# Attention and two feed-forward layers on one core: signs restored by a bit, a shorter weight split, pooling placed by the plan

## The chip, the cores and the metric

The kernel runs on one NeuronCore of one Trainium2 chip. The number that counts is the device time of one execution in microseconds (us); a run's profile shows the span, from the first to the last instruction of the core, which is slightly shorter. Engines are named as in the profile: PE (TensorE, matmuls), PEld (its weight loads), DVE (VectorE), ACT (ScalarE), POOL (GpSimd) and SP (SyncE, whose queue issues all DMAs here).

## The reference

Three layers follow each other on 4608 tokens (8 batches of 576). Inputs are of both kinds: q, k and v are 32-bit floats, the weights come as 64-bit floats.

```python
k_p = k.reshape(B, H, 72, 8, 64).mean(axis=3)        # pool keys and values by 8
v_p = v.reshape(B, H, 72, 8, 64).mean(axis=3)
attn = softmax(q @ k_p.T / 8)                        # 8 heads of 64
x = (attn @ v_p)  -> [4608, 512]
h = x @ w_in                                         # 512 -> 1024
solu = h * softmax(h)
ln = (solu - mean) / sqrt(var + 1e-6) * g_ln
x = ln @ w_out                                       # 1024 -> 512
h = x @ w2_in                                        # 512 -> 2048
out = (h * sigmoid(1.702 * h)) @ w2_out              # 2048 -> 512
```

## The kernel before, in words

The program has two parts. The first does attention and the first layer (w_in, w_out), and prepares the weights of the second layer (w2_in, w2_out) beside them; its 18 pairs of 128-token tiles leave their result in DRAM (y_dram). The second part runs the second layer over 12 blocks of 384 tokens, with a scheme of seven products in place of eight; its instruction order is written out by hand and the diff doesn't touch it. Every fp32 operand of a matmul is held as a high and a low fp16 half, so that each product is three passes.

**The weights.** They arrive as 64-bit words, in tiles called raw with the two 32-bit words of each number side by side: hw, the high word, and lw, the low word. A fp32 value is put together from them in pieces of 128x512. In `joined` (first layer) and `values_of` (second layer) ACT takes the sign of the high word (tile sg, fp16), converts the low word, and rescales the high word; DVE shifts and joins the two into a positive fp32 word; and POOL multiplies by the sign. The first layer has 16 such pieces, 8 of w_in and 8 of w_out. For these `first_half` then has ACT scale the value into a tile val, ACT write its high fp16 half (tile w1i or w1o), and POOL or DVE subtract to get the low half. The second layer has 32 pieces in 16 quarters (`Quarter`): there POOL's product goes into w_f, out of which POOL makes sums and differences, ACT the high and POOL the low halves, and SP stores both to DRAM. The sign tiles come from a ring of four (SG).

**The pooling.** `half` loads one half of a batch's keys or values (tile half, 128x2x72x8) and `total` adds each group of eight: on DVE it is one reduction, on POOL three additions of halves. The table KV_POOL sends two of the 32 halves to POOL: the second half of keys 0 and the second of values 1.

**Each tile of attention** goes through psx (scores, PE), a maximum, a subtraction, an exponential and a sum (DVE and ACT on tile e), a product with the reciprocal (POOL or DVE), a split into st (ACT and POOL), a DMA transpose into aT, the product with the values in PSUM tile psv (PE), and its split into xT (ACT and DVE). **The first layer** goes through psh (PE, xT times w1i), a maximum, an exponential, a product (tt) and a square on DVE and ACT, statistics on POOL (q, r, a, mean), a split into zs (ACT and POOL), a DMA transpose into zT, psy (PE, zT times w1o), and y.

**The order in the first part** is made by a planner in the kernel's own code (class `Plan`) as the program is built. Each piece of work is a strand, a generator that yields operations with a cost for each engine that may take it. Over and over the planner takes the operation that could begin first by its clocks (one for each engine in `plan.free`, one for the DMAs), shifted a little by its due time, and emits it; the engines then work in that order. V, A, G mean DVE, ACT and POOL alone; VG lets the planner choose between POOL and DVE, with 3000 ns against DVE; `there` emits nothing and holds a strand until its data are there by the planner's clocks. A changed cost or engine therefore changes the order of all that follows in the first part.

Of the kernel before, what the change touches and what calls it, by code (L numbers as in the profile page):

```python
# [8 lines left out]
F32 = mybir.dt.float32  # L9
F16 = mybir.dt.float16  # L10
I32 = mybir.dt.int32
U32 = mybir.dt.uint32
AF = mybir.ActivationFunctionType
ALU = mybir.AluOpType
# [4 lines left out]
P = 128  # L19
# [18 lines left out]
UW = 256  # L38
WC = 512
# [29 lines left out]
DUE_MAX_IN = -10000  # L69
DUE_MAX_OUT = 20000  # L70

RAWS = 4
SG = 4
TTS = 4
V_TOP = 2.0 ** 14

TOP3 = 2.0 ** -29 * (1 - 2.0 ** -23)
A_TOP = 2.0 ** 14
LN_UP = 2.0 ** 10
CI_LEAST, CI_MOST = 2.0 ** -50, 2.0 ** 40  # L80
# [11 lines left out]
NS = 7  # L92
# [79 lines left out]
class Plan:  # L172
# [30 lines left out]
    def drop(self, *tiles):  # L203
        for t in tiles:
            del self.ring_of[t.name]
# [75 lines left out]
def moe_kernel(ctx: ExitStack, tc: tile.TileContext, qT, kT, vT, w_in, w_out, g_ln, w2_in, w2_out, eye, outT):  # L281
# [135 lines left out]
    with ExitStack() as ph:  # L417
# [4 lines left out]
        kv = tc.alloc_tile_pool(name="kv", bufs=2, side="right")  # L422
# [12 lines left out]
        plan = Plan()  # L435
        start, drop = plan.start, plan.drop
# [4 lines left out]
        def there(*ins):  # L441

            return Op(("none",), lambda engine: None, [], ins, {"none": 0})
# [46 lines left out]
        def V(name, *args, **kw):  # L490
            return op(("dve",), name, args, kw)

        def G(name, *args, **kw):
            return op(("pool",), name, args, kw)

        def VG(name, *args, **kw):
            return op(("pool", "dve"), name, args, kw)

        def A(**kw):
            return op(("act",), "activation", (), kw)  # L500
# [89 lines left out]
        def values_of(raw, up, dst, begun=None):  # L590

            hw, lw = raw[:, :, 1], raw[:, :, 0]
            sg = yield New(kv, [P, WC], F16, "sg", bufs=SG)
            if begun is not None:
                begun.append(sg)
            yield A(out=sg, in_=hw.bitcast(F32), func=AF.Sign)
            yield A(out=lw.bitcast(U32), in_=lw.bitcast(U32), func=AF.Copy, scale=TOP3, bias=-0.49999)
            yield lambda: (up.name, up.offset) in upped
            yield A(out=hw.bitcast(F32), in_=hw.bitcast(F32), func=AF.Copy, scale=up)
            yield V(  # L600
                "scalar_tensor_tensor", out=lw, in0=hw, scalar=3, in1=lw, op0=ALU.logical_shift_left,
                op1=ALU.bitwise_or,
            )
            d = yield from dst()
            yield G("tensor_tensor", out=d, in0=sg, in1=lw.bitcast(F32), op=ALU.mult)
            drop(sg)

        def raw_new(q, n):
            return New(kv, [P, q, n, 2], I32, "raw", "raw", RAWS)

# [19 lines left out]
        def joined(raw, measured):  # L630
# [3 lines left out]
            yield A(out=sg, in_=hw.bitcast(F32), func=AF.Sign)  # L634
            yield A(out=lw.bitcast(U32), in_=lw.bitcast(U32), func=AF.Copy, scale=TOP3, bias=-0.49999)
            yield measured
# [8 lines left out]
        def first_half(raw, measured, scaled, up, k, c, his):  # L645

            yield from joined(raw, measured)
            yield scaled
            val = yield New(kv, [P, NS, UW], F32, "val", "w_f", 2)
            v = val.rearrange("p s f -> p (s f)")[:, :WC]  # L650
            hi, lo = (x[:, k, c] for x in his)
            yield A(out=v, in_=raw[:, :, 0].bitcast(F32), func=AF.Copy, scale=up)
            yield A(out=hi, in_=v, func=AF.Copy)
            yield VG("tensor_tensor", out=lo, in0=v, in1=hi, op=ALU.subtract)
            drop(val)

        def halves(n):
            return [slice(j * WC, (j + 1) * WC) for j in range(n // WC)]
# [73 lines left out]
            scaled = start(scale(), due)  # L732
            yield until(*[start(part(i), due + 4 * i) for i in range(n)])

        KV_POOL = {("k", 0): 1, ("v", 1): 1}

        def spans(t):

# [7 lines left out]
        def total(engine, out, x):  # L746

            if engine is V:
                yield V("tensor_reduce", out=out, in_=x, axis=AX.X, op=ALU.add)
                return  # L750
            for n in (4, 2):
                yield G("tensor_tensor", out=x[..., 0:n], in0=x[..., 0:n], in1=x[..., n : 2 * n], op=ALU.add)
            yield G("tensor_tensor", out=out, in0=x[..., 0], in1=x[..., 1], op=ALU.add)
# [4 lines left out]
        def half(kind, b, j, src, dst):  # L758

            raw = yield New(kv, [P, 2, SP, NPOOL], F32, "half", bufs=3)  # L760
            begun[kind][b] += 1
            yield D(raw.rearrange("p a s o -> p a (s o)"), src[b][:, 2 * j : 2 * j + 2])
            yield from total(G if KV_POOL.get((kind, b)) == j else V, dst[:, 2 * j : 2 * j + 2], raw)
            drop(raw)

        def pooled(kind, b, src, due):
# [48 lines left out]
        def attention(t):  # L815
# [42 lines left out]
            yield V("tensor_reduce", out=rs, in_=e, axis=AX.X, op=ALU.add)  # L858
            yield A(out=rs, in_=rs, func=AF.Copy, scale=1.0 / A_TOP, bias=1e-9 / A_TOP)
            yield V("reciprocal", rs, rs)  # L860
# [33 lines left out]
            turned_x = ps.rearrange("p (k t) -> p k t", t=P)  # L894
            yield A(out=xT[:, 0:KM], in_=turned_x, func=AF.Copy, scale=1.0 / A_TOP)
            yield V(
# [270 lines left out]
        begun = {kind: [0] * B for kind in "kv"}  # L1167
# [18 lines left out]
        def due(t):  # L1186
            return FIRST_STEP + STEP * t
# [21 lines left out]
        for b in range(1, B):  # L1209
            d = due(b * S // P + LEAD_KV) if b > 1 else DUE_KV1  # L1210
# [13 lines left out]
        for u in range(len(chunks) // 2):  # L1224
            d = FIRST_STEP + LAG_W2 + 2 * u * STEP_W2
# [254 lines left out]
```

## Time and profile before

| what | us |
|---|---|
| median of 3 runs | 1255.61 |
| lowest and highest run | 1253.86, 1258.69 |
| profiled execution, its own time | 1253.29 |
| profiled execution, its span | 1251.5 |
| granted TensorE clock, mean of the span | 0.986 |
| PE busy in the span | 1143.5 (91%) |
| ACT, DVE, POOL busy in the span | 766.5, 730.9, 664.7 |

Busy time is the sum of an engine's instructions in a stretch; what is left of the stretch is idle time. A row of the waits says who stood still, for whom, how long in total, how often, and the longest time. In a row of the timeline or of the groups the part in brackets, or after the second bar, is the idle time of that engine just before the instruction, and what ended it.

### The profile page before, as it was taken

Reading aid. Unit: us, or ns where it says so; the run is one execution under the profiler, and the core shown is the slowest. Engines: PE = TensorE matmul, PEld = TensorE weight load, DVE = VectorE, ACT = ScalarE, POOL = GpSimd, SP = SyncE. Lnnn points to the kernel's source line nnn. Section 1 sums busy time; section 2 is a strip of 40 time slices with the busy share of each in tenths; the row PEclk is TensorE's granted clock in tenths of the full one; section 3 lists DMA queues with packets and bytes.
Section 4 is the critical chain, followed back from the end, with each engine's and each line's share of the span. In section 5 each row is a group of like instructions: output and inputs, shape, how many; then the busy total and the mean of one; then the engine's idle time right before and its main releaser. Section 6 shows DMA issues by size and latency. Waiting matters only on the chain.

```text
span 1251.5 us, 27586 instructions
## 1 busy us (share of the span) xinstructions
PE 1143.5 (91%) x11678; PEld 989.6 (79%) x11678; DVE 730.9 (58%) x1153; ACT 766.5 (61%) x1073; POOL 664.7 (53%) x696
## 2 busy tenths in 40 slices
PE   2778998899999999889999999999999999999998
PEld 2335665576666666789999999999999898999998
DVE  7898877587677843136455454637272737364543
ACT  6998998788789855345445353627263536454552
POOL 5887998687879953424333352525262515243331
PEclk9989999899999999999999999999999999999999
DMA  9979999999989698470101010100011010101000
GB/s 324 302 205 240 269 270 256 248 231 248 256 206 234 164 230 236 109 270 8 46 14 39 14 40 20 33 27 27 27 33 46 7 46 8 46 7 46 14 14 26
DMA packets 246524, 152.85 MB, mean 122 GB/s; under 512 B 163584, under 2 KB 226176, under 8 KB 244096
## 3 DMA queue, kind: packets, MB, share of 16 engines
q1 hardware_dynamic: 246400, 151.09, 45.5%
q8 instruction: 91, 1.49, 0.5%
q14 instruction: 33, 0.27, 0.1%
HBM read 77.66 MB, written 33.55 MB: 89 GB/s over the span
## 4 chain that ended last, share of the span: by engine, by line
PE 30%; POOL 12%; DVE 8%; ACT 8%; issue 5%; DMA 0%; ACTq 0%; POOLq 0%
PE bank_a L1290 18%; PE bank_d L1290 8%; ACT w_g L1325 6%; DVE g L1337 5%; POOL w_g L336 3%; PE bank_b L1290 3%; POOL w_g L335 3%; POOL w_g L333 2%; POOL w_g L334 2%; PE psy L512 2%; ACT g L1334 1%; DVE c L1303 1%; POOL zs L475 1%; DVE w_g L333 0%; ACT c L1300 0%
## 5 line engine op out<-in xcount | busy, mean ns | idle before, releaser
L1290 PEld LDWEIGHTS <-w2i 128*128 128x128 f16 x4032 | 337.4, 98 | 34.3 <-issue 33.7
L1290 PEld LDWEIGHTS <-w2o 128*128 128x128 f16 x4032 | 335.0, 98 | 7.4 <-issue 6.8
L333 POOL TENSOR_TENSOR w_g<-w_g 128x384 f32<-128x384 f32 x36 | 43.6, 1211 | 379.3 <-ACT w_g L1325 379.3
L1290 PE MATMUL bank_a<-ys,w2i 128*128 128x192 f16 x2304 | 215.1, 247 | 27.1 <-ACT c L1300 25.0
L512 PE MATMUL psh<-w1i,xT 128*128 128x512 f16 x864 | 205.8, 389 | 8.9 <-DVE mean L475 8.2
L1290 PE MATMUL bank_a<-g,w2o 128*128 128x192 f16 x2304 | 206.0, 246 | 1.0
L512 PE MATMUL psy<-zT,w1o 128*128 128x256 f16 x1728 | 196.8, 273 | 8.8 <-ACT y L475 8.8
L512 PEld LDWEIGHTS <-w1o 128*128 128x128 f16 x1728 | 167.9, 98 | 35.8 <-issue 10.3
L1337 DVE SCALAR_TENSOR_TENSOR g<-w_g,gu_b,g 128x1152 f16<-128x1152 f32 (+1 forms) x96 | 169.1, 1782 | 24.5 <-ACT g L1334 24.4
L512 PEld LDWEIGHTS <-xT 128*128 128x128 f16 x864 | 84.4, 100 | 103.9 <-issue 13.8
L1300 ACT ACTIVATE c<-bank_a 128x384 f32<-128x384 f32 x192 | 91.7, 484 | 116.4 <-PE bank_a L1290 113.1
L1334 ACT ACTIVATE g<-w_g,gu_b 128x1152 f16<-128x1152 f32 (+1 forms) x96 | 132.9, 1408 | 39.4 <-POOL w_g L336 39.0
L1303 DVE SCALAR_TENSOR_TENSOR c<-bank_d,c 128x384 f32<-128x384 f32 x96 | 53.3, 555 | 134.4 <-ACT c L1300 99.5
L475 POOL TENSOR_TENSOR zs<-tt,zs 128x1024 f16<-128x1024 f32 x36 | 77.4, 2149 | 59.7 <-ACT zs L475 59.5
L1290 PE MATMUL bank_d<-ys,w2i 128*128 128x192 f16 x1152 | 107.5, 249 | 0.3 <-DVE c L1303 0.3
L1290 PE MATMUL bank_d<-g,w2o 128*128 128x192 f16 x1152 | 102.4, 246 | 3.0 <-DVE g L1337 3.0
L1325 ACT ACTIVATE w_g<-c,ch_b 128x1536 f32<-128x1536 f32 x48 | 75.3, 1568 | 36.8 <-DVE c L1303 36.7
L1300 ACT ACTIVATE c<-bank_a,co_b 128x384 f32<-128x384 f32 x47 | 26.9, 573 | 108.6 <-PE bank_a L1290 108.6
L512 PE MATMUL psx<-kbd,qt 128*128 128x144 f32 (+1 forms) x320 | 46.3, 306 | 24.6 <-ACT raw_z L475 12.7
L512 PEld LDWEIGHTS psx<-kbd,qt 128*128 128x128 f32 (+1 forms) x320 | 41.4, 193 | 29.4 <-issue 12.7
L475 POOL TENSOR_TENSOR lo<-w_f,hi 128x512 f16<-128x512 f32 (+1 forms) x46 | 62.2, 1365 | 2.7 <-ACT hi L475 2.3
L475 DVE TENSOR_REDUCE hmx<-psh 128x1 f32<-128x1024 f32 x36 | 43.7, 1214 | 34.1 <-PE psh L512 34.1
(189 smaller groups left out, 1693.1 us busy)
## 6 DMA issues: line engine op xcount, KB each, us to landing
raw<-w_out SPq DMA_DIRECT2D x12, 1024.0 KB, 6.9
raw<-w_in SPq DMA_DIRECT2D x10, 1024.0 KB, 8.0
half<-kT SPq DMA_DIRECT2D x16, 576.0 KB, 5.4
half<-vT SPq DMA_DIRECT2D x16, 576.0 KB, 5.5
qt<-qT SPq DMA_DIRECT2D x36, 256.0 KB, 3.9
y_dram<-y SPq DMA_DIRECT2D x36, 256.0 KB, 2.8
y<-y_dram SPq DMA_DIRECT2D x48, 192.0 KB, 3.2
outT<-c SPq DMA_DIRECT2D x48, 192.0 KB, 1.9
```

What stands on the lines that cost most here:

```text
L333: eng.tensor_tensor(out=w[:, 1], in0=q[:, Q12], in1=q[:, Q11], op=ALU.subtract)
L334: eng.tensor_tensor(out=w[:, 2], in0=q[:, Q22], in1=w[:, 1], op=ALU.subtract)
L335: eng.tensor_tensor(out=w[:, 0], in0=q[:, Q22], in1=q[:, Q12], op=ALU.subtract)
L336: eng.tensor_tensor(out=w[:, 3], in0=q[:, Q21], in1=w[:, 2], op=ALU.subtract)
L475: getattr(eng, name)(*args, **kw)
L512: nc.tensor.matmul(*p[:3], start=p[3], stop=p[4])
L1290: nc.tensor.matmul(bank[:, q], self.weight(p, q, kk, w), self.data(p, kk, i), start=(first and q == 0 and kk == 0 and w == 0 and i == 0), ...
L1300: nc.scalar.activation(out=self.c[:, i], in_=bank, func=AF.Copy, scale=self.scale)
L1303: nc.vector.scalar_tensor_tensor(out=self.c[:, i], in0=bank, scalar=self.scale, in1=self.c[:, i], op0=ALU.mult, op1=ALU.add)
L1325: nc.scalar.activation(out=self.w[:, 0:4], in_=self.c, func=AF.Gelu_apprx_sigmoid, scale=self.ch)
L1334: nc.scalar.activation(out=self.g[:, 0, s], in_=self.w[:, s], func=AF.Copy, scale=self.gu)
L1337: nc.vector.scalar_tensor_tensor(out=self.g[:, 1, s], in0=self.w[:, s], scalar=self.gu, in1=self.g[:, 0, s], op0=ALU.mult, op1=ALU.subtract,)
```

## The change

- In `values_of` (second layer) the sign tile, ACT's sign instruction and POOL's multiplication go. In their place DVE takes the sign bit of the rescaled high word, joins it to the positive word, and writes w_f. `joined` (first layer) keeps the sign tile and the multiplication.
- In `first_half` the tile val goes: ACT writes the high half straight from the joined word with the scale, and DVE alone writes the low half from the joined word, the scale and the high half, in one instruction.
- The second half of values 1 is no longer fixed to POOL. For all batches after the first, `half` waits until its data are there by the planner's clocks and then takes POOL if POOL's clock plus 1300 ns lies before DVE's, and DVE otherwise.

```diff
+POOL_MORE = 1300
...
+SIGN = -(2 ** 31)
...
         def values_of(raw, up, dst, begun=None):
 
             hw, lw = raw[:, :, 1], raw[:, :, 0]
-            sg = yield New(kv, [P, WC], F16, "sg", bufs=SG)
             if begun is not None:
-                begun.append(sg)
-            yield A(out=sg, in_=hw.bitcast(F32), func=AF.Sign)
+                begun.append(True)
             yield A(out=lw.bitcast(U32), in_=lw.bitcast(U32), func=AF.Copy, scale=TOP3, bias=-0.49999)
...
             d = yield from dst()
-            yield G("tensor_tensor", out=d, in0=sg, in1=lw.bitcast(F32), op=ALU.mult)
-            drop(sg)
+
+            yield V(
+                "scalar_tensor_tensor", out=d.bitcast(I32), in0=hw, scalar=SIGN, in1=lw, op0=ALU.bitwise_and,
+                op1=ALU.bitwise_or,
+            )
...
             yield from joined(raw, measured)
             yield scaled
-            val = yield New(kv, [P, NS, UW], F32, "val", "w_f", 2)
-            v = val.rearrange("p s f -> p (s f)")[:, :WC]
             hi, lo = (x[:, k, c] for x in his)
-            yield A(out=v, in_=raw[:, :, 0].bitcast(F32), func=AF.Copy, scale=up)
-            yield A(out=hi, in_=v, func=AF.Copy)
-            yield VG("tensor_tensor", out=lo, in0=v, in1=hi, op=ALU.subtract)
-            drop(val)
+            v = raw[:, :, 0].bitcast(F32)
+            yield A(out=hi, in_=v, func=AF.Copy, scale=up)
+            yield V("scalar_tensor_tensor", out=lo, in0=v, scalar=up, in1=hi, op0=ALU.mult, op1=ALU.subtract)
...
-        KV_POOL = {("k", 0): 1, ("v", 1): 1}
+        KV_POOL = {("k", 0): 1}
...
-            yield from total(G if KV_POOL.get((kind, b)) == j else V, dst[:, 2 * j : 2 * j + 2], raw)
+            yield there(raw)
+            free = plan.free["pool"] + POOL_MORE < plan.free["dve"]
+            yield from total(G if (b == 0 and KV_POOL.get((kind, b)) == j) or (b and free) else V, dst[:, 2 * j : 2 * j + 2], raw)
```

## Rows read from the trace of the kernel before

**Rows 1.** The page, part 1: busy time, share of span, instructions by engine.

```profile
PE 1143.5 (91%) x11678; PEld 989.6 (79%) x11678; DVE 730.9 (58%) x1153; ACT 766.5 (61%) x1073; POOL 664.7 (53%) x696
```

**Rows 2.** Busy times by stretch: length, PE, PEld, DVE, ACT, POOL, clock, DMA.

```profile
31.00:125.00 94.00, 70.75 (x491) 40.86 (x491) 82.19 (x157) 85.43 (x143) 75.57 (x88) 0.91 0.96 249
125.00:440.00 315.00, 297.42 (x2404) 205.58 (x2402) 234.65 (x439) 270.58 (x428) 274.88 (x341) 0.99 0.98 237
440.00:539.00 99.00, 86.41 (x698) 65.40 (x696) 29.41 (x47) 45.26 (x60) 37.20 (x56) 1.00 0.69 185
```

**Rows 3.** The same view, the second part of the program.

```profile
539.00:1252.00 713.00, 681.10 (x8062) 670.74 (x8061) 360.55 (x467) 343.60 (x407) 260.86 (x188) 0.99 0.11 37
```

**Rows 4.** Waits of PE, 20 to 125 us.

```profile
PE psv L512 <- DMA aT<-st: 12.9, 4, 7.3
PE psh L512 <- DVE mean L475: 7.3, 3, 3.7
```

**Rows 5.** Waits of PE, 125 to 440 us.

```profile
PE psv L512 <- DVE xT L475: 10.3, 5, 5.2
```

**Rows 6.** Timeline, 56 to 92 us: start, duration, engine, instruction.

```profile
72.08 1.27 POOL L475 TENSOR_TENSOR st<-e,st 128x576 f16<-128x576 f32 x1
...
77.14 1.07 PE L512 MATMUL psv<-aT,vst 128*64 128x128 f16 x16 [7.31 <-DMA aT<-st]
```

**Rows 7.** Timeline, 208 to 218 us.

```profile
213.25 1.35 DVE L475 TENSOR_REDUCE kp<-half 128x144 f32<-128x1152 f32 x1 [1.47 <-DMA half<-kT]
...
216.38 0.64 PE L512 MATMUL psv<-aT,vst 128*64 128x128 f16 x16 [1.99 <-DVE xT L475]
```

**Rows 8.** Timeline, 234 to 248 us.

```profile
235.57 2.75 PE L512 MATMUL psh<-w1i,xT 128*128 128x512 f16 x12
...
242.67 1.35 DVE L475 TENSOR_REDUCE kp<-half 128x144 f32<-128x1152 f32 x1 [5.77 <-DMA half<-kT]
...
245.07 0.68 DVE L475 SCALAR_TENSOR_TENSOR xT<-psv,xT 128x512 f16<-128x512 f32 x1
...
245.81 0.80 PE L512 MATMUL psv<-diag,ones 128*128 128x128 f32 x2 [5.21 <-DVE xT L475]
```

**Rows 9.** Timeline of PE alone, 244 to 256 us.

```profile
246.40 4.50 PE L512 MATMUL psh<-w1i,xT 128*128 128x512 f16 x12
```

**Rows 10.** Busy times by stretch, columns as in rows 2.

```profile
247.00:249.00 2.00, 2.00 (x7) 0.65 (x5) 1.90 (x8) 1.77 (x5) 0.00 (x0) 0.50 0.75 170
```

**Rows 11.** Groups of ACT, 31 to 125 us: busy us, mean ns.

```profile
L475 ACT ACTIVATE val<-raw,w1o_gs 128x512 f32<-128x512 f32 x8 | 5.9, 750 | 0.6 <-POOL w1o L475 0.6
L475 ACT ACTIVATE w1i<-val 128x512 f16<-128x512 f32 x8 | 4.8, 626 | 0.1
L475 ACT ACTIVATE w1o<-val 128x512 f16<-128x512 f32 x8 | 4.8, 620 | 0.0
```

**Rows 12.** Groups of POOL, 31 to 125 us.

```profile
L475 POOL TENSOR_TENSOR w1i<-val,w1i 128x512 f16<-128x512 f32 x8 | 10.0, 1266 | 0.2 <-ACT w1i L475 0.2
L475 POOL TENSOR_TENSOR w1o<-val,w1o 128x512 f16<-128x512 f32 x8 | 9.6, 1212 | 0.5 <-ACT w1o L475 0.5
```

**Rows 13.** Groups of DVE, 31 to 125 us.

```profile
L475 DVE SCALAR_TENSOR_TENSOR raw<-raw 128x512 int32<-128x512 int32 x12 | 11.2, 939 | 0.0
```

**Rows 14.** Tile raw, whole span: ns shortest/median/longest, first and last start.

```profile
L475 DVE SCALAR_TENSOR_TENSOR raw<-raw x44: 634/743/2366, 26.5 to 424.8; 128x512 int32<-128x512 int32 x44
```

**Rows 15.** Busy times of instructions on tile sg: length, ACT, POOL.

```profile
125.00:440.00 315.00, 19.24 (x29) 38.79 (x30) 0.99 0.98 237
```

**Rows 16.** Groups of DVE, 125 to 440 us.

```profile
L475 DVE SCALAR_TENSOR_TENSOR raw<-raw 128x512 int32<-128x512 int32 x30 | 29.1, 986 | 0.9 <-ACT raw L475 0.8
...
L475 DVE TENSOR_TENSOR e<-e,rs 128x576 f32<-128x576 f32 x8 | 12.5, 1563 | 0.0
```

**Rows 17.** Busy times of instructions on tile half: length, DVE, POOL.

```profile
31.00:125.00 94.00, 10.74 (x8) 2.54 (x3) 0.91 0.96 249
125.00:440.00 315.00, 23.95 (x18) 0.00 (x0) 0.99 0.98 237
```

## The prediction

> **What bounds the kernel now.** I read four views, from the whole to the single wait. The page's busy times come first [rows 1]: PE is busy for 91% of the span and no other engine for more than 61%, so on average PE is the bound. That average hides the stages, so the busy times by stretch come next. From 539 us on, the second layer runs, PE is busy 681 of 713 us [rows 3], and the diff doesn't reach its instructions. All that can change lies ahead of 539 us, and there what counts is the time in which PE stands still, since PE's own work is the same before and after. PE is idle 94 - 70.8 = 23.2 us from 31 to 125 us (stage 1), 315 - 297.4 = 17.6 us from 125 to 440 us (stage 2), and 99 - 86.4 = 12.6 us from 440 to 539 us, where the last tiles drain and weight preparation is about over [rows 2]. Whatever idle time goes in stages 1 and 2 brings the end forward one for one, because PE has only its remaining work to do after it.
>
> Stage 1 is close to full on every engine that feeds PE: ACT 85.4, DVE 82.2 and POOL 75.6 of 94 us. Stage 2 has POOL at 274.9, ACT at 270.6 and DVE at 234.7 of 315 us: PE leads by some 20 us, so most of what the others save there buys nothing [rows 2].
>
> The waits of PE say what ends last. In stage 1 they are mainly two: 12.9 us for the transposed attention weights, which come by DMA from st, and 7.3 us for DVE to free the PSUM of the hidden layer [rows 4]. The longest, 7.31 us, ended at 77.14; POOL had begun the split that feeds such a transpose only at 72.08 [rows 6]. In stage 2 it is the split xT on DVE, 10.3 us in five waits [rows 5]. Two of those five have a cause that the change touches. At 213.25 and 242.67 DVE stood before a pooling reduction whose transfer was late (1.47 and 5.77 us); xT was queued behind it, and PE waited 1.99 and 5.21 us for xT [rows 7, 8]. [...] The two places cost PE 1.99 + 5.21 + 1.75 = 8.95 us.
>
> **The first layer's split**, 16 pieces, all in stage 1. ACT did two instructions, val at 0.75 us and the half at 0.62 us, and now does one. The new one reads the strided word with a scale as val did, and writes fp16 as the half did; between 0.62 and 0.75 us I take 0.75, so ACT saves 16 x 0.62 = 9.9 us [rows 11]. POOL loses 10.0 + 9.6 = 19.6 us [rows 12]. DVE gets 16 instructions that the trace doesn't show. The nearest row is the join of the words, also two inputs, also strided, also 512 wide: 0.634 at the least, 0.743 in the median [rows 14], 0.939 in this stage's mean [rows 13]. So 10.1 to 15.0 us; I take the median, 11.9 us, because POOL, which the longer ones stand beside, will be less busy. What queues behind them on DVE is the maximum, the product and xT of the tiles, for which PE waits.
>
> **The second layer's sign**, 32 pieces, 30 of them in stage 2, two just before it. ACT loses 19.2 us and POOL 38.8 us there [rows 15]. DVE gets 30 instructions of the same nearest kind: 30 x 0.634 = 19.0 to 30 x 0.986 = 29.6 us [rows 14, 16]; by the median 22.3 us. With the ring of sign tiles gone, ACT may begin a piece earlier; that moves work and adds none. The holding operation in the pooling emits nothing.
>
> **The pooling.** A half costs 10.74 / 8 = 1.34 us on DVE and 2.54 us in three additions on POOL [rows 17]. Stage 1 has eight on DVE and one on POOL, stage 2 has eighteen on DVE. How many will move hangs on the plan's clocks, which the trace doesn't show: none to all. I take half, four and nine: DVE saves 5.4 and 12.0 us, POOL gets 10.2 and 22.9 us. No DMA is added or dropped, but loads that follow a half's buffer can move in SP's queue.
>
> **Loads after.** Stage 1: ACT 85.4 - 9.9 = 75.5, POOL 75.6 - 19.6 + 10.2 = 66.2, DVE 82.2 + 11.9 - 5.4 = 88.7 us of 94. Stage 2: ACT 270.6 - 19.2 = 251.4, POOL 274.9 - 38.8 + 22.9 = 259.0, DVE 234.7 + 22.3 - 12.0 = 245.0 us of 315. Moreover POOL can take back what DVE did for it in stage 2, eight products of e, 12.5 us at 1.56 us each [rows 16]. So stage 2 gets room on the two fullest engines, and stage 1 trades a full ACT for a full DVE.
>
> **The sum.** In stage 1, POOL is 19.6 / 75.6 = 26% lighter before any pooling comes to it, and I let a quarter of the 12.9 us of transpose waits go, -3.3 us; DVE is 88.7 / 82.2 = 8% fuller, and its 7.3 us of waits grow by as much, +0.6 us. In stage 2 the two places of 8.95 us go if those reductions move to POOL or fall elsewhere in the new order; I count two thirds, -6.0 us. For the rest of stage 2 (17.6 - 7.2 = 10.4 us) and the drain I count nothing: there the lighter engines were already ahead of PE, and if that cover were gone it is at most that much. Together -8.7 us. The profiled execution took 1253.3 us (span 1251.5 and 1.8 around it), so 1244.6 by its measure; it lay 2.3 us below the median of 1255.6, so the forecast is 1246.9 us.
>
> **A price that may be wrong.** The join on DVE takes 0.634 us at its shortest and 0.986 us in stage 2's mean, up to 2.37 us [rows 14, 16], though its shape never changes: something makes it wait, by up to a third of its mean. All 48 new DVE instructions read two operands from SBUF, as it does. [...] This is the second rival.
>
> **Rivals.** (1) *Nothing that counts.* PE is the bound of stage 2, and the plan is a new one: waits that go at 216 and 246 us come back at other places, and stage 1's savings on ACT are eaten by DVE. For it speaks how far PE already leads; against it, that POOL and ACT lose 58 and 29 us together over both stages. 1255.6 us, give or take 5. (2) *DVE becomes the bound of stage 1.* At 0.939 us each the 16 splits cost 15.0 us; with four halves moved DVE has 82.2 + 15.0 - 5.4 = 91.8 us, 6.4 more than the fullest engine now. The stage now takes 94 / 85.4 = 1.10 us for each us of its fullest engine, so +7.0 us; if no half moves at all (the change then doesn't do what it says), DVE has 97.2 us, +13 us. Stage 2 gives nothing back in this case, as its new DVE work meets POOL's. 1262.6 us, up to 1268.6. It decides from about 89 us of DVE work in stage 1, just above what I reckon. (3) *The feed was the limit after all.* With POOL and ACT lighter, all 12.9 us of transpose waits go but 2, and all 8.95 us of the two places: about -20 us, 1235.6 us.
>
> **How the numbers follow.** The forecast has a chance of 0.50, with its own range of 1240 to 1252 (3.6 to 15.6 us off); rival 1 has 0.22, rival 2 0.18, rival 3 0.10. A measurement of this kernel tells about 0.5%, 6.3 us, from no change, so the bounds are 1249.3 and 1261.9. Of the forecast 0.39 lies below the lower bound and 0.11 between; rival 3 is below; rival 1 is between but for 0.02 above; rival 2 is above. Faster 0.49, same 0.31, slower 0.20. The range is 1235 to 1263 us: it leaves out about half of rival 2 and a little under half of rival 3.
>
> **What would show it.** In the profile after: 48 new DVE instructions at 0.74 us, 0.9 or more if rival 2 holds; ACT some 10 us lighter in stage 1 and 19 us in stage 2; no sg rows in the second layer; about half of the kp and vp rows on POOL. Right is the forecast if PE's waits for xT behind a late pooling transfer are gone and its waits for aT are shorter; wrong if the waits of PE for DVE in stage 1 grow past 8 us, or if the sum of PE's idle time up to the first instructions of the second layer stays as it is. Since the order of the whole first part is made anew, a single long wait that I can't foresee, of the 5 to 7 us seen here, would be enough to spoil it.

## The result and the profile after

The changed kernel takes 1266.39 us in the median of 20 runs (1254.61 to 1276.01), the kernel before 1256.12 us in 20 runs beside it (1251.89 to 1264.61). The ratio is 1.0075, with a 95% interval of 1.0052 to 1.0098: slower by 9.4 us, where 1246.9 us was forecast. Two of the 20 runs, the profiled one of 1275.63 us among them, count as slow (over 1.5% above the fastest run) and are left out of the ratio, which is therefore below 1266.39 / 1256.12 = 1.0082. The profiled execution lies some 9 us over the median, so its rows show where time went, and the ratios of the runs say how much; its main readings are repeated below on the traces of other kernels.

Part 1 of the page of the changed kernel:

```profile
PE 1151.2 (90%) x11678; PEld 992.2 (78%) x11678; DVE 754.4 (59%) x1192; ACT 743.1 (58%) x1039; POOL 629.2 (49%) x655
```

Against [rows 1] ACT is 23.4 and POOL 35.5 us lighter and DVE 23.5 us heavier. PE stands still for 1273.8 - 1151.2 = 122.6 us of the span where it had been 1251.5 - 1143.5 = 108.0, and the same 11,678 matmuls take 7.7 us longer. Busy times by stretch of the changed kernel, columns as in [rows 2]:

```profile
31.00:125.00 94.00, 70.56 (x458) 40.27 (x454) 81.09 (x157) 74.10 (x123) 57.40 (x70) 0.84 0.93 229
125.00:440.00 315.00, 281.56 (x2237) 193.62 (x2235) 247.48 (x448) 243.48 (x391) 242.49 (x305) 0.96 0.98 234
```

Against [rows 2], stage 1 has the same busy time of PE with 33 matmuls fewer in it, at a lower granted clock (0.84, before 0.91), and DVE is not fuller but a little emptier (81.1, before 82.2). In stage 2 PE works 15.9 us less than before. PE's waits in the two stages, for [rows 4, 5]:

```profile
PE psv L514 <- DMA aT<-st: 12.2, 4, 5.0
PE psh L514 <- DVE mean L477: 8.3, 4, 3.6
...
PE psv L514 <- DVE xT L477: 25.6, 6, 8.5
```

Two hardly move. The wait for xT in stage 2 grows from 10.3 to 25.6 us, and its longest from 5.2 to 8.5 us. The timeline of the changed kernel around that longest one:

```profile
337.51 0.75 POOL L477 TENSOR_TENSOR mean<-mean,a 128x2 f32<-128x2 f32 x1
337.52 8.29 DVE L477 SCALAR_TENSOR_TENSOR raw<-raw 128x512 int32<-128x512 int32 x2
...
338.21 3.86 POOL L477 TENSOR_TENSOR lo<-w_f,hi 128x512 f16<-128x512 f32 x3
...
342.03 2.12 POOL L477 TENSOR_TENSOR zs<-tt,zs 128x1024 f16<-128x1024 f32 x1
344.11 1.15 POOL L477 TENSOR_TENSOR e<-e,rs 128x576 f32<-128x576 f32 x1
...
347.22 0.67 DVE L477 SCALAR_TENSOR_TENSOR xT<-psv,xT 128x512 f16<-128x512 f32 x1
...
347.95 1.06 PE L514 MATMUL psv<-aT,vst 128*64 128x128 f16 x16 [8.55 <-DVE xT L477]
```

Two joins on DVE, a shape that is done in 0.64 us at the shortest, take 8.29 us, the second of them 7.69. POOL is ending a small instruction (mean) when the second join begins, and then runs five two-input instructions without a gap from 338.21 to 345.26; the join ends some half a microsecond after the last of them. Behind it in DVE's queue stands xT, whose input ACT had written by 338.70, and PE waits 8.55 us. Tile raw and the pieces w_f over the whole span, for [rows 14] (ns shortest/median/longest):

```profile
L477 DVE SCALAR_TENSOR_TENSOR raw<-raw x44: 641/685/7692, 26.0 to 441.9; 128x512 int32<-128x512 int32 x44
L477 DVE SCALAR_TENSOR_TENSOR w_f<-raw x32: 674/686/1804, 130.4 to 443.8; 128x512 int32<-128x512 int32 x32
```

The median is even lower than before (0.743); the tail is what changed. In stage 2 the groups of DVE, for [rows 16], have the joins at a mean of 1.124 us (before 0.986) and the new signs at 0.882:

```profile
L477 DVE SCALAR_TENSOR_TENSOR raw<-raw 128x512 int32<-128x512 int32 x31 | 34.4, 1124 | 0.1
L477 DVE SCALAR_TENSOR_TENSOR w_f<-raw 128x512 int32<-128x512 int32 x31 | 27.2, 882 | 1.2 <-POOL lo L477 0.9
```

### The profile page after: what moved, and what is told of

Same layout as the page of the kernel before. It is cut to its first block, busy times and chain, and to the rows that moved or that the text cites. A ratio compares the mean times of both kernels' runs of the same rounds, so it can differ in the third digit from the quotient of the medians.

```text
span 1273.8 us, 27549 instructions
## 1 busy us (share of the span) xinstructions
PE 1151.2 (90%) x11678; PEld 992.2 (78%) x11678; DVE 754.4 (59%) x1192; ACT 743.1 (58%) x1039; POOL 629.2 (49%) x655
## 4 chain that ended last, share of the span: by engine, by line
PE 40%; DVE 19%; POOL 16%; ACT 11%; DMA 7%; issue 6%; SPq 1%; ACTq 0%; POOLq 0%; DVEq 0%
PE bank_a L1292 17%; PE bank_d L1292 7%; PE psy L514 7%; ACT w_g L1327 6%; DVE g L1339 6%; PE psh L514 5%; POOL w_g L338 3%; POOL w_g L337 3%; POOL w_g L335 2%; PE bank_b L1292 2%; DMA half<-kT 2%; POOL w_g L336 2%; POOL lo L477 2%; DMA aT<-st 2%; DVE hmx L477 1%
## 5 line engine op out<-in xcount | busy, mean ns | idle before, releaser
L514 PE MATMUL psh<-w1i,xT 128*128 128x512 f16 x864 | 213.0, 400 | 10.5 <-DVE mean L477 9.1
L514 PEld LDWEIGHTS <-w1o 128*128 128x128 f16 x1728 | 168.7, 98 | 35.5 <-issue 10.1
L477 POOL TENSOR_TENSOR lo<-w_f,hi 128x512 f16<-128x512 f32 (+1 forms) x48 | 65.5, 1380 | 3.9 <-DMA w2i_dram<-lo 3.8
L514 PE MATMUL psx<-kbd,qt 128*128 128x144 f32 (+1 forms) x320 | 47.0, 309 | 22.3 <-ACT raw_z L477 12.2
L1305 DVE SCALAR_TENSOR_TENSOR c<-bank_b,c 128x384 f32<-128x384 f32 x48 | 26.6, 555 | 66.0 <-ACT c L1302 49.2
```

Of the source, the lines that this page charges most:

```text
L477: getattr(eng, name)(*args, **kw)
L514: nc.tensor.matmul(*p[:3], start=p[3], stop=p[4])
L1305: nc.vector.scalar_tensor_tensor(out=self.c[:, i], in0=bank, scalar=self.scale, in1=self.c[:, i], op0=ALU.mult, op1=ALU.add)
```

## The experiments

Ratios are those of the runs to the kernel before on the same chip, with the 95% interval. The suspects were: late transfers in front of xT (A in the texts), DVE instructions with two inputs in SBUF that POOL holds up (B), DVE as the bound of stage 1 (C, rival 2 of the prediction), loads of weights ahead of transposes in SP's queue (D), and the new order as such (E); later also the place of DVE work among that of the tiles.

**One part at a time.** Each of the first three has one part of the diff on the kernel before; the fourth leaves out the pooling.

`sign_alone`:

```diff
-            yield A(out=sg, in_=hw.bitcast(F32), func=AF.Sign)
...
-            yield G("tensor_tensor", out=d, in0=sg, in1=lw.bitcast(F32), op=ALU.mult)
+            yield V(
+                "scalar_tensor_tensor", out=d.bitcast(I32), in0=hw, scalar=SIGN, in1=lw, op0=ALU.bitwise_and,
+                op1=ALU.bitwise_or,
+            )
```

> Only the second layer's sign moves to DVE. Theory B (the DVE instructions with two SBUF inputs get blocked by POOL's): this part alone makes most of the loss, 1262 to 1267 us, with joins or sign instructions on DVE of several us in the profile. Theory A (the order is made anew and DVE stands before late pooling transfers with xT queued behind): any part alone may do it or not; 1250 to 1258 us here, as ACT and POOL are relieved and the pooling is not touched. Theory C (DVE is the bound of 31 to 125 us through the first layer's split): 1251 to 1256 us.

`split_alone`:

```diff
-            yield A(out=v, in_=raw[:, :, 0].bitcast(F32), func=AF.Copy, scale=up)
-            yield A(out=hi, in_=v, func=AF.Copy)
-            yield VG("tensor_tensor", out=lo, in0=v, in1=hi, op=ALU.subtract)
+            yield A(out=hi, in_=v, func=AF.Copy, scale=up)
+            yield V("scalar_tensor_tensor", out=lo, in0=v, scalar=up, in1=hi, op0=ALU.mult, op1=ALU.subtract)
```

> Only the first layer's split is shortened. Theory C: 1260 to 1265 us, with PE's idle time from 31 to 125 us up by 5 or more. Theories A and B: 1250 to 1258 us, the stage to 125 us unchanged or better by a few us.

`pool_alone`:

```diff
-            yield from total(G if KV_POOL.get((kind, b)) == j else V, dst[:, 2 * j : 2 * j + 2], raw)
+            yield there(raw)
+            free = plan.free["pool"] + POOL_MORE < plan.free["dve"]
+            yield from total(G if (b == 0 and KV_POOL.get((kind, b)) == j) or (b and free) else V, dst[:, 2 * j : 2 * j + 2], raw)
```

> Only the pooling's choice and its holding operation. Theory A: as the holding operation and the new choice move the reductions in DVE's order, this alone moves the time by more than 5 us, either way, and PE's waits for xT stand behind kp<-half rows. Theories B and C: within 4 us of the kernel before, since at most a few halves change engine.

`split_sign` has both of the first two edits.

> The whole change without the pooling's part. Theory B: 1262 to 1267 us, as the whole change. Theory A: 1250 to 1258 us, since the pooling's order is what puts late transfers ahead of xT. Theory C: 1260 to 1265 us.

Measured: sign_alone 1.0059 [1.0037, 1.0081], split_alone 1.0051 [1.0032, 1.0070], pool_alone 1.0014 [0.9994, 1.0035], split_sign 1.0082 [1.0057, 1.0108]. Both parts lose by themselves. Their sum, 1.1%, is above the 0.82% that the two cost together, but the intervals don't tell the two apart. The pooling does nothing that can be measured: POOL has two of the 32 halves in pool_alone and in the changed kernel, as many as the table gave it before.

The sign's loss shows in stage 2. Busy times by stretch of sign_alone:

```profile
31.00:125.00 94.00, 71.74 (x495) 42.50 (x491) 83.74 (x158) 85.24 (x143) 73.93 (x87) 0.91 0.95 248
125.00:440.00 315.00, 288.30 (x2276) 198.77 (x2275) 246.16 (x450) 246.77 (x391) 251.08 (x313) 0.96 0.95 233
```

Stage 1 is close to that of [rows 2]; in stage 2 PE works 9.1 us less. And it has the same accident as the changed kernel, at another time (timeline of sign_alone):

```profile
324.57 8.29 DVE L476 SCALAR_TENSOR_TENSOR raw<-raw 128x512 int32<-128x512 int32 x2
...
335.00 1.06 PE L513 MATMUL psv<-aT,vst 128*64 128x128 f16 x16 [8.56 <-DVE xT L476]
```

But the loss doesn't need such an accident. split_sign loses as much as the changed kernel, and no join or sign of its takes over 2.35 us (tiles raw and w_f); PE's longest wait for xT in stage 2 is 4.4 us there.

```profile
L476 DVE SCALAR_TENSOR_TENSOR raw<-raw x44: 637/690/2158, 26.0 to 432.7; 128x512 int32<-128x512 int32 x44
L476 DVE SCALAR_TENSOR_TENSOR w_f<-raw x32: 674/692/2346, 128.4 to 434.6; 128x512 int32<-128x512 int32 x32
```

**The changed kernel with one suspect taken away.** The planner doesn't see these edits, so the order stays that of the changed kernel.

`no_late_load`, in `total`:

```diff
+                if b > 1:
+                    add.emit = lambda engine: nc.vector.tensor_reduce(out=out, in_=there_now, axis=AX.X, op=ALU.add)
```

> The changed kernel with its order of instructions kept as it is; the pooling reductions on DVE for batches from the third on read a tile that has long been there instead of the half that was just loaded (keys and values of these batches are wrong by that; the loads still run). So DVE no longer stands before a late pooling transfer. Theory A (late transfers ahead of xT on DVE): 1250 to 1257 us, PE's waits for xT near 172 and 258 us gone. Theory B (DVE blocked by POOL): 1262 to 1267 us. Theory D (the 1 MB weight load one place ahead of a transpose in the DMA queue, found in the split-alone profile at 97 us): 1262 to 1267 us, the standstill of all engines near 104 us stays.

`no_block`, in `values_of`:

```diff
+            join.emit = lambda engine: nc.vector.tensor_reduce(
+                out=lw.bitcast(F32), in_=w1i[1][:, 0, :WC].unsqueeze(2), axis=AX.X, op=ALU.max
+            )
...
+            sign.emit = lambda engine: nc.vector.tensor_reduce(
+                out=d, in_=lw.bitcast(F32).unsqueeze(2), axis=AX.X, op=ALU.max
+            )
```

> The changed kernel in its own order; the 64 word joins and signs of the second layer on DVE become reductions of the same 512 numbers with one SBUF input (the second layer's weights are wrong by that). Theory B: 1252 to 1260 us, no DVE instruction of these over 0.8 us, the 8.55 us wait of PE near 348 us gone. Theories A and D: 1262 to 1267 us.

`load_behind`, in the planner:

```diff
+            if s.item.held:
+                self.late.append(s.item)
+            else:
+                s.item.emit(engine)
+            if s.item.turn:
+                for late in self.late:
+                    late.emit("sp")
+                self.late = []
```

> The changed kernel with the order of compute instructions kept; each load of a second-layer weight quarter is issued behind the next DMA transpose instead of ahead of it. Nothing is left out. Theory D: 1256 to 1262 us, the standstill near 104 us shorter by 3 us or more and the clock of 31 to 125 us above 0.84. Theories A and B: 1264 to 1268 us, or worse if the joins now wait for their words.

`all_three` has the three edits together.

> The three edits of these runs together (keys, values and second-layer weights wrong as said there). If A, B and D are each part of it and nothing else is: below 1250 us, PE idle from 125 to 440 us under 12 us. If the loss is in the new order for other reasons: 1258 to 1266 us.

Measured: no_late_load 1.0068 [1.0044, 1.0092], no_block 0.9990 [0.9972, 1.0008], load_behind 1.0325 [1.0296, 1.0354], all_three 1.0251 [1.0226, 1.0276]. With 64 instructions made reductions of one input, and nothing else, the whole loss is gone; it is no longer told from the kernel before. The reductions leave out the join and the sign, so the second layer's weights are wrong, but its length doesn't hang on them: from its first product with w2o to the start of the last it takes 681.4 us in the kernel before, 680.3 in the changed one and 679.3 in no_block. Nor do the joins' reductions wait for ACT's high word; all idle time before the joins was 0.1 us in stage 2 of the changed kernel. The late loads are worth less than their interval, and no_late_load, whose order is that of the changed kernel, has its accident once more: two joins of 8.28 us, PE waiting 8.55 us for xT. The edit to the queue was a miss: loads that go out later are themselves waited for (up to 560 us DVE waited 25.5 us for raw<-w_out, 6.1 in the changed kernel, and PE's waits for xT came to 33.7 us, the longest 14.5), and in all_three that hides all else. Tile raw of no_block, where lines 604 and 614 are the reductions:

```profile
L604 DVE TENSOR_REDUCE raw<-w1i x32: 634/677/682, 132.1 to 426.0; 128x512 f32<-128x512 f16 x32
L614 DVE TENSOR_REDUCE w_f<-raw x32: 667/678/720, 133.7 to 426.7; 128x512 f32<-128x512 f32 x32
```

Their medians are those of the instructions they replace, 0.68 us; what has gone is the tail, of 7.69 and 1.80 us. PE's wait for xT in stage 2 is 14.6 us, where it is 19.9 in no_late_load and 25.6 in the changed kernel, though the order is the same in all three.

**Which of the 64.** `no_block_sign` has the edit `sign.emit` of no_block alone, and `before_no_block` has `join.emit` alone, on the kernel before.

> The changed kernel in its own order; only the 32 new sign instructions become reductions with one SBUF input, the joins stay (the weights lose their signs). If the new instructions themselves are what is blocked: 1253 to 1258 us. If it is the join, which the change only put at a worse place: 1260 to 1266 us, and the 7.7 us join near 338 us is still there.

> The kernel before in its own order; the 32 joins of the second layer on DVE become reductions of 512 numbers with one SBUF input (the second layer's weights are wrong by that). If blocking is the change's own cost (its 32 new instructions set it off): within 3 us of the kernel before, as its longest join takes 2.4 us. If blocking costs the kernel before as much: 1240 to 1247 us, and then it doesn't explain the difference.

Measured: 1.0008 [0.9989, 1.0027] and 0.9956 [0.9938, 0.9974]. Making only the 32 new instructions one-input takes the changed kernel from 1.0075 to 1.0008. Groups of DVE in stage 2 of no_block_sign, and its tile raw:

```profile
L477 DVE SCALAR_TENSOR_TENSOR raw<-raw 128x512 int32<-128x512 int32 x32 | 26.9, 851 | 0.1
L610 DVE TENSOR_REDUCE w_f<-raw 128x512 f32<-128x512 f32 x32 | 21.5, 678 | 2.8 <-POOL lo L477 2.5
...
L477 DVE SCALAR_TENSOR_TENSOR raw<-raw x44: 640/686/1949, 26.0 to 424.4; 128x512 int32<-128x512 int32 x44
```

The signs take 0.678 us where they took 0.882. The joins, still with two inputs, come down too, from a mean of 1.124 to 0.851 us, and the block of 7.69 us, which had fallen on a join, is gone: the longest join there takes 1.95 us. That the join and POOL's run of instructions no longer met in that way, with other durations ahead of them, is my reading and was not shown. What the signs cost PE shows in its busy time in stage 2, here of no_late_load, split_sign and no_block_sign:

```profile
125.00:440.00 315.00, 289.83 (x2320) 201.41 (x2319) 257.35 (x466) 250.52 (x404) 250.64 (x320) 0.97 0.98 237
```

```profile
125.00:440.00 315.00, 287.79 (x2294) 199.16 (x2292) 251.38 (x456) 246.73 (x397) 249.27 (x311) 0.97 0.97 237
```

```profile
125.00:440.00 315.00, 295.27 (x2361) 204.24 (x2360) 244.85 (x476) 257.20 (x412) 248.52 (x320) 0.98 1.00 243
```

With two-input signs PE gets to 288 to 290 us of work (sign_alone: 288.3), with one-input signs to 295.3 (no_block: 296.0).

The kernel before pays a like price already: its own 32 joins of the second layer, made one-input, give back 0.44%, 5.5 us, which lies between the two ranges expected. At most 0.9 us of it is the wait for ACT's high word [rows 16], which the reductions don't have. This also changes how no_block is to be read: half of its 64 instructions are joins that the kernel before has too. With the joins relieved in both, the changed kernel is still some 0.3% behind, 0.9990 against 0.9956. That part of the loss is not the blocking of these 64.

**Why the split loses.** The same device on the split, on split_alone (`split_no_block`):

```diff
+            low.emit = lambda engine: nc.vector.tensor_reduce(out=lo, in_=hi.unsqueeze(2), axis=AX.X, op=ALU.max)
```

> The first layer's split alone, in its own order; its 16 new DVE instructions become reductions with one SBUF input (the low halves are wrong by that). If blocking costs in 31 to 125 us too: 1254 to 1258 us. If the loss there is the order of the DMAs (theory D): 1260 to 1264 us as split alone.

And two loads of split_alone set one transpose further back in SP's queue, by the edit of load_behind for these two alone (`split_two_behind`):

```diff
+                load.held = i == 1
...
+                load.held = self.n == 3
```

> The first layer's split alone, with the order of compute instructions kept and two 1 MB weight loads of the DMA queue moved one place back, behind the attention transpose that they stood before (the second w_out load near 32 us, the fourth load of w2_in near 97 us). Nothing is left out. Theory D: 1254 to 1259 us, the waits of PE for aT near 45 and 107 us (2.76 and 5.19 us) shorter by 2 us or more each. Otherwise: 1260 to 1264 us.

Measured: 1.0064 [1.0049, 1.0080] and 1.0070 [1.0043, 1.0097]. Neither takes the loss away, so both suspects fall for this part. The next four, on the kernel before, separate the new order from the work. `split_old_order` emits the split's instructions where the old ones stood; the order of all others is that of the kernel before:

```diff
+            one.emit = lambda engine: nc.scalar.activation(out=hi, in_=word, func=AF.Copy, scale=up)
+            two.emit = lambda engine: None
+            low.emit = lambda engine: nc.vector.scalar_tensor_tensor(
+                out=lo, in0=word, scalar=up, in1=hi, op0=ALU.mult, op1=ALU.subtract
+            )
```

> The first layer's split alone, but planned with the old costs, so that every other instruction stands in the order of the kernel before; ACT writes the high half where it wrote val, and DVE the low half where POOL did. Nothing is left out. If the split alone lost through the order that the plan made of it (theory E): 1249 to 1256 us. If 16 more instructions on DVE from 31 to 125 us cost it (rival 2 of the prediction): 1259 to 1264 us.

`low_half_dve` takes the low halves from the planner's choice and does nothing else:

```diff
-            yield VG("tensor_tensor", out=lo, in0=v, in1=hi, op=ALU.subtract)
+            yield V("tensor_tensor", out=lo, in0=v, in1=hi, op=ALU.subtract)
```

> The kernel before with one letter changed: the subtraction that makes the low half in the first layer may go to DVE only; ACT keeps both its instructions, the plan is made anew. If work put on DVE in 31 to 125 us is the cost: 1258 to 1266 us, PE idle there above 25 us. If it is not: 1250 to 1257 us.

`neutral_order_1` and `neutral_order_2` change no work but a number of the planner each, for two other orders:

```diff
-LAG_HIDDEN = 0
+LAG_HIDDEN = 500
...
-    LAG = {"pe": 197, "dve": 150, "act": 160, "pool": 75, "dma": 950}
+    LAG = {"pe": 197, "dve": 155, "act": 160, "pool": 75, "dma": 950}
```

> The kernel before with the due times of the hidden layer 500 ns later: the same work, another order. Theory E (any new order moves the time by as much as the split did): more than 4 us off the kernel before, either way. If order matters little: 1252 to 1257 us.

> The kernel before with the planner's lag behind DVE at 155 instead of 150 ns: the same work, another order. As neutral_order_1: theory E more than 4 us off, either way; otherwise 1252 to 1257 us.

Measured: split_old_order 1.0086 [1.0061, 1.0110], low_half_dve 1.0082 [1.0062, 1.0103], neutral_order_1 0.9976 [0.9955, 0.9996], neutral_order_2 0.9994 [0.9980, 1.0008]. The two other orders cost nothing. 16 low halves on DVE cost 0.8%, with the rest of the split or without, and in split_old_order with the order of all else as before; that is even more than split_alone's 0.51%, and split_old_order's 1266.66 us lies above the range expected of it. Timeline of low_half_dve around its longest wait:

```profile
75.24 1.23 DVE L475 TENSOR_REDUCE hmx<-psh 128x1 f32<-128x1024 f32 x1
...
76.98 1.45 DVE L475 TENSOR_TENSOR w1o<-val,w1o 128x512 f16<-128x512 f32 x2
...
88.77 1.21 ACT L475 ACTIVATE he<-psh,nm,h_sc 128x1024 f32<-128x1024 f32 x1
...
92.25 0.68 DVE L475 TENSOR_TENSOR w1o<-val,w1o 128x512 f16<-128x512 f32 x1
...
94.12 1.44 PE L512 MATMUL psh<-w1i,xT 128*128 128x512 f16 x3 [17.94 <-DVE mean L475]
```

A tile's maximum (hmx) was done at 76.47, its exponential (he) came on ACT 12 us later, and its product (tt) on DVE at 92.84, for 1.22 us: ACT and DVE did weight pieces in between, low halves among them. Until that product frees the PSUM of psh, PE stands still, for 17.94 us; the longest wait of this kind had been 3.7 us [rows 4].

The last two put the low halves on POOL, `split_low_pool` on split_alone and `no_block_low_pool` on no_block, with one edit:

```diff
-            yield V("scalar_tensor_tensor", out=lo, in0=v, scalar=up, in1=hi, op0=ALU.mult, op1=ALU.subtract)
+            yield G("tensor_tensor", out=lo, in0=v, in1=hi, op=ALU.subtract)
```

> The kernel before with the first layer's split made straight from the joined word, but with each of the 16 low halves on POOL as the two-input subtraction that the kernel before has there (1.16 us) and not on DVE; it leaves the factor out of the low half, so that half's values are not the reference's. ACT still has 16 instructions less. If the split loses because of the 16 instructions on DVE in stage 1, the loss of split_alone (ratio 1.0051) goes: a ratio of 0.997 to 1.001 and DVE busy for some 69 to 73 us less 16 x 0.75 in that stage than split_alone counted against the same work. If it loses because ACT's removed instruction or the shifted stage 1 upsets what follows, whichever engine has the low half, the ratio stays at 1.004 to 1.009.

> The changed kernel with both remedies: the 64 joins and signs of the second layer as one-input reductions (they leave out the join and the sign of those weights) and the 16 low halves of the first layer on POOL as a two-input subtraction without the factor (that half's values are not the reference's). If two-input instructions on DVE that POOL's chains hold up, and the low halves on DVE, are together the whole loss, the ratio is 0.991 to 0.996, below no_block's 0.999 by what the split cost and near or below before_no_block's 0.9956. If the low halves' place does not matter, it stays at no_block's 0.997 to 1.001.

Measured: 0.9982 [0.9958, 1.0006] and 1.0057 [1.0029, 1.0086]. The first bears out the cause: the split with its low halves on POOL loses nothing. The second is a miss. It was to beat no_block and is slower by 0.7%. The joins and signs of its second layer are short (0.63 to 0.71 us), so it isn't the blocking of stage 2 that came back. One join of the first layer takes 7.52 us, at 31.47 us, but so does one in split_low_pool, which loses nothing. What it has less of is work done in stage 1. Busy times of that stretch in split_low_pool, no_block and no_block_low_pool, in this order:

```profile
31.00:125.00 94.00, 66.97 (x441) 38.66 (x437) 80.23 (x144) 72.62 (x119) 71.80 (x83) 0.93 0.88 225
```

```profile
31.00:125.00 94.00, 68.55 (x437) 38.17 (x437) 78.83 (x152) 71.56 (x116) 56.47 (x66) 0.84 0.91 229
```

```profile
31.00:125.00 94.00, 65.10 (x410) 36.13 (x406) 79.33 (x141) 70.84 (x117) 65.30 (x72) 0.87 0.88 222
```

In these 94 us the last does 410 matmuls, no_block 437, the kernel before 491 [rows 2]. But no_block and split_low_pool lose nothing with some 50 matmuls fewer than before, so the state at 125 us doesn't settle the end alone; stage 2 can make it good. Why POOL as the place of the low halves helps in one order and not in the other stays open. Nor do two orders that cost nothing show that none does: this one loses 0.57% with neither of the two causes in it. So the kernels whose order was planned anew (sign_alone, split_alone, low_half_dve, split_low_pool) say less than those that keep an order and change its instructions (no_block, no_block_sign, before_no_block, split_old_order).

## Why the prediction was wrong

**What bounds the kernel.** Right in kind: PE leads and its standing still counts; from [rows 2, 3] to the rows after, the second layer keeps its length. "PE's own work is the same before and after" holds in number only: in the two profiled executions the same matmuls take 7.7 us more, at a mean granted clock of 0.975 against 0.986. Part of that is no cost of the change: kernels that lose nothing also lie above 1143.5 us (no_block_sign 1146.2, no_block 1146.8, neutral_order_1 1149.1).

**The second layer's sign: the step that failed.** Two sentences did it: "by the median 22.3 us", and, for the rest of stage 2, "I count nothing". The joins of [rows 16] and the signs together were to take 29.1 + 22.3 = 51.4 us of DVE; they took 34.4 + 27.2 = 61.6 us (34.3 + 28.1 = 62.4 in sign_alone). I had named DVE's queue, with a tile's xT behind the new instruction, for the first layer's split alone, and for neither part priced a new instruction or a join that is held up while PE waits behind it. PE's waits for xT grew by 15.3 us, one of them to 8.55. The test is no_block_sign: 32 instructions with one input take the ratio from 1.0075 to 1.0008, some 8.4 us of the 9.4. How that divides between the one long block and the many short ones isn't separated; split_sign loses 0.82% without the long one, so the loss doesn't hang on the single long wait that the prediction's last sentence feared.

What the traces show of the long joins is where they lie. The longest of the kernel before, 2.37 us for a shape of 0.634 [rows 14], runs beside the first of two POOL instructions that follow each other without a gap, and ends 0.55 us after that one (timeline of the kernel before):

```profile
113.43 2.14 POOL L475 TENSOR_TENSOR zs<-tt,zs 128x1024 f16<-128x1024 f32 x1 [1.19 <-ACT zs L475]
113.75 2.37 DVE L475 SCALAR_TENSOR_TENSOR raw<-raw 128x512 int32<-128x512 int32 x1
115.53 1.73 POOL L475 TENSOR_TENSOR st<-e,st 128x576 f16<-128x576 f32 x1
```

In the changed kernel it is 7.69 us for a join among five POOL instructions in a row; in no_block it is never over 0.72 us for the reductions in their place. That POOL holds the two-input instructions up is my reading of these places: no run took POOL's instructions alone away, and the reductions differ from them in the operation as well as in the number of inputs. The prediction had set a longer duration of such instructions beside the sum as a rival of 0.18 and taken the median for the sum.

**The first layer's split: failed too.** Its 11.9 us for DVE came to 14.5 (the w1o pieces 8 at a mean of 1.028 us, the w1i pieces 8 at 0.78), and its consequence was sized as "+0.6" on the waits. Stage 1 did not get fuller on DVE, it did less: 81.1 us where 88.7 was reckoned, as other work slid out of the stage. So rival 2's condition, DVE full from 89 us, never came true, but its price did (1262.6 to 1268.6 us; measured 1266.39); for stage 1 that is luck. Of the signs of being wrong one did come: PE's waits for DVE's mean in stage 1 were 8.3 us, past the 8 that were named. What the runs put in place of a full engine is the engine that has the pieces: the low halves cost 0.8% on DVE with no other work changed (low_half_dve), and nothing on POOL (split_low_pool). That it is their position between a tile's dependent steps is read from one timeline and not tested. The kernel before had given the planner the choice with 3000 ns against DVE, and all 16 went to POOL [rows 12]; the change takes that choice away. Blocking, the two loads and the order as such were each tried and fell (split_no_block, split_two_behind, split_old_order). What stays open is why it doesn't show in no_block_sign (1.0008), which has the split on DVE as well. The joins are faster there than in the kernel before, 0.851 us against 0.986, which may hide some of it, as in no_block; that was not tested. In the profiled execution of split_alone PE's idle time is even that of before (1258.9 - 1150.7 = 108.2 us against 108.0), and its busy time 7.2 us longer. Part of that is in stage 1; the busy times from 80 to 125 us, of split_alone and of the kernel before:

```profile
80.00:125.00 45.00, 33.13 (x212) 19.81 (x213) 36.21 (x67) 35.88 (x59) 29.17 (x39) 0.81 1.04 241
```

```profile
80.00:125.00 45.00, 38.05 (x250) 22.69 (x248) 38.26 (x72) 40.06 (x64) 33.80 (x49) 0.93 1.03 254
```

The granted clock is 0.81 in the one and 0.93 in the other. But no_block_sign, which loses nothing, has 0.81 there too, with fewer matmuls, so the lower clock in this stretch is not by itself the loss:

```profile
80.00:125.00 45.00, 33.64 (x207) 20.21 (x207) 35.76 (x68) 35.55 (x56) 29.36 (x41) 0.81 1.07 237
```

**The pooling.** "I take half, four and nine" failed outright: no half beyond the two of before went to POOL. It cost nothing either, and the loads reckoned with it (POOL 33.1 us fuller, DVE 17.4 us emptier) never came.

**The two places of late transfers, -6.0.** They didn't go. Another pair came, a reduction that waited 5.98 us and one that waited 6.53 (lines of the changed kernel, timeline from 250 us):

```profile
253.24 2.79 DVE L477 TENSOR_REDUCE kp<-half 128x144 f32<-128x1152 f32 x2 [6.53 <-DMA half<-kT]
...
257.81 0.80 PE L514 MATMUL psv<-diag,ones 128*128 128x128 f32 x2 [6.66 <-DVE xT L477]
```

No run shows the 1.75 us in the two places' 8.95 to be the price of a wait. What the rows have is twelve matmuls in 4.50 us [rows 9] and in 2.75 [rows 8], and a granted clock of 0.50 from 247 to 249 us [rows 10]; behind the new wait of 6.66 us the changed kernel has 0.50 too, from 258 to 262 us. The whole term was oversized in any case: with no such wait from the third batch on (no_late_load) the ratio falls from 1.0075 to 1.0068, 0.9 us, well within the intervals.

**The transpose waits, -3.3.** 12.9 became 12.2 us: POOL and ACT were 18 and 11 us lighter in stage 1, and the aT waits did not care. Rival 3 falls with it. Rival 1's 1255.6 us is where the kernel ends without the blocking (no_block, 0.9990), by the number only, since the joins of the kernel before are relieved there too. The range ended at 1263, 3.4 us short.

## What to carry to other kernels

Before an instruction is moved to DVE, look at the longest duration of its like in the trace and not at the median, and at what stands behind it in the queue: here 32 more instructions with a median of 0.69 us cost some 8 us, because they and their like took as long as 7.69 us ahead of an operation for which PE waits. An engine with room by its busy time may be no free place for work: 16 low halves on DVE cost 0.8%, in one trace between a tile's dependent steps. A form with one SBUF input on DVE is worth looking for even in the kernel before: 32 one-input reductions in place of its joins gave back 0.44%. The reductions here only stand in for such a form, since they leave the work out.

## What the runs showed of the hardware that had not been expected

A two-input DVE instruction lasted to the end of a whole chain of POOL instructions and not only of one of its members: five instructions in a row, 338.21 to 345.26, one join of 7.69 us. In split_low_pool it is seven, without a gap from 30.55 to 38.48, and a join of the first layer of 7.51 us (timeline):

```profile
30.55 4.48 POOL L475 TENSOR_TENSOR w1i<-raw_z,w1i 128x512 f16<-128x512 f32 x4
31.52 7.51 DVE L475 SCALAR_TENSOR_TENSOR raw<-raw 128x512 int32<-128x512 int32 x1
...
37.33 1.15 POOL L475 TENSOR_TENSOR raw<-sg,raw 128x512 f32<-128x512 f16 x1
...
39.69 1.04 PE L512 MATMUL psh<-w1i,xT 128*128 128x512 f16 x2 [5.66 <-DVE xT L475]
```

There too PE waited behind it, 5.66 us for xT, and yet that kernel ends no later than the one before (0.9982): one such wait early in the program can be made good.

It doesn't always go on to the end of the chain. In the changed kernel's trace POOL runs without a gap from 278.05 to 284.92, and a join and a sign come through in 2.14 and 1.53 us meanwhile (timeline):

```profile
278.05 4.34 POOL L477 TENSOR_TENSOR lo<-w_f,hi 128x512 f16<-128x512 f32 x3
...
279.23 2.14 DVE L477 SCALAR_TENSOR_TENSOR raw<-raw 128x512 int32<-128x512 int32 x1
281.41 1.53 DVE L477 SCALAR_TENSOR_TENSOR w_f<-raw 128x512 int32<-128x512 int32 x1
282.35 2.57 POOL L477 TENSOR_TENSOR zs<-tt,zs 128x1024 f16<-128x1024 f32 x1
```

What decides between the two was not looked for.

The spread of the runs also grew with the change, from 12.7 us (1251.89 to 1264.61) to 21.4 us; its cause was not looked for.
